# Cached sliding-window attention on one core: three pairs of value tiles loaded as 32 KB rows, and a new order of the loads

## The chip, the cores and the metric

One core of one Trainium2 chip runs the whole program. The metric is the device time of one execution in microseconds (us); the span of a profile is the part of it between first and last instruction, some 1.8 us shorter. A run of a program on one core repeats within some 0.3 us here, so most experiments were timed in five rounds beside the kernel before on the same chip. All ratios are the mean time of one kernel's fast runs over that of the other's of the same rounds, so not quite the ratio of the medians that are quoted. A run over 1.5% above the fastest of its kernel counts as slow, the others as fast; slow runs are named and left out of the times.

## The reference, cut to what matters

One decoding step of grouped-query attention over the last 512 positions of a cache: 32 batches, 32 query heads, 8 key-value heads, head size 128, bf16.

```python
W = min(4096, max(256, Sk // 4))                      # 512
q = (x @ wq).reshape(B, Sq, Hq, Dh) ...               # [32, 32, 1, 128]
k = repeat(k_cache[:, :, Sk - W:, :], 4, axis=1)
v = repeat(v_cache[:, :, Sk - W:, :], 4, axis=1)
p = softmax(einsum("bhqd,bhkd->bhqk", q, k) * Dh ** -0.5)
o = einsum("bhqk,bhkd->bhqd", p, v)
out = o.transpose(...).reshape(B, Sq, Hq * Dh) @ wo   # [32, 1, 512]
```

33.5 MB of K, 33.5 MB of V, 4.2 MB of wq and 4.2 MB of wo have to be read once, 75.5 MB in all, for very little arithmetic.

## The kernel before: what the change touches

K and V are cut into 16 tiles each of 2 MB: 128 rows (batch, head, quarter of the window) of 16 KB, one row per partition. Tile 2q+1 continues the rows of tile 2q, so two tiles of one pair are 32 KB in a row in memory. There are three K buffers and four V buffers. One queue (SyncE, SP) issues all loads but the small x in a fixed order; an issue waits until its buffer is free. K needs its two transposes on VectorE (T) before its buffer is free; V needs its 64 matmuls on TensorE.

Every load of 128 rows leaves 16 completion increments in the trace, as many as the page counts DMA engines; they are read here as one from each engine when its share has landed. The first is that of the earliest engine, the last that of the latest; their distance is called the spread here. Steps are counted from one load's first increment to the next one's. An engine that took no instruction fetch is called undisturbed.

```python
NK = 3
NV = 4
DMA_ORDER = (
    "K0 K1 K2 V0 K3 K4 V1 K5 K6 K7 V2 K8 K9 V3 K10 V4 K11 K12 V5 K13 K14 V6 K15 V7 V8 V9 V10 V11 V12 "
    "V13 V14 V15"
).split()
# ... PE_ORDER, DVE_ORDER, ACT_ORDER: fixed orders of the compute steps (cut)

def cache_rows(cache, m):
    q, e = divmod(m, 2)
    rows = cache[4 * q:4 * q + 4, :, SK - W:, :].rearrange("b g (s r) d -> (b g) s (r d)", s=KS)
    return rows[:, :, e * CR * DH:(e + 1) * CR * DH]

@block.sync
def _(sp):
    sp.dma_start(w_sb[:, 2:4, :]..., wq_rows[:, wq_half:]).then_inc(sem_wq[1], 16)   # second half of wq
    for name in DMA_ORDER:
        n = int(name[1:])
        if name[0] == "K":
            if n >= NK:
                sp.wait_ge(dve_T, 2 * (n - NK + 1))
            sp.dma_start(K_sb[:, n % NK]..., cache_rows(k_cache, n)).then_inc(sem_k[n % NK], 16)
        else:
            if n >= NV:
                sp.wait_ge(pe_PV, n - NV + 1)
            sp.dma_start(V_sb[:, n % NV]..., cache_rows(v_cache, n)).then_inc(sem_v[n % NV], 16)
    sp.wait_ge(pe_PV, 2 * Z_HOME.rindex("w") + 2)
    # ... nine loads of wo, the output store (cut)

def pv(m):                                  # TensorE, one value tile
    # ... (cut)
    pe.wait_ge(sem_v[m % NV], 16 * (m // NV + 1))
    for r in range(CR):                     # CR = 64
        ins = pe.matmul(O_ps[:, q % 2, 0:P], lhsT=V_sb[:, m % NV, r, :], rhs=z_of(q)[:, :, x0 + r, :],
                        start=(e == 0 and r == 0), stop=(e == 1 and r == CR - 1), tile_position=(0, 0))
    ins.then_inc(pe_PV, 1)
```

## Time and profile before

| | kernel before |
|---|---|
| time, median | 187.69 us (3 runs), 187.67 us over 6 runs |
| span of the profiled execution | 185.9 us |
| DMA packets | 6304, 75.80 MB |
| one 2 MB transfer behind another, undisturbed engine | 4.893 us |
| eighth of nine wo transfers, named by the chain, and ninth landed | 182.67 and 182.99 us |
| first and last of the 16 DMA engines at the end | 3.2 us apart |

### The profile page before, as it was taken

The page shows a single profiled execution, that of the slowest core. Times are in us where ns is not written, and L with a number is a line of the kernel's source. Part 1 is how long each engine was busy: PE and PEld are TensorE (multiplying, and loading weights), DVE is VectorE, ACT ScalarE, POOL GpSimd, SP SyncE. Part 2 cuts the span into 40 slices and gives each one's busy share as a digit, 9 for nine tenths or more (in the row PEclk, how much of TensorE's full clock was granted, in tenths as well). Part 3 has the DMA queues.
Part 4 walks back from the last instruction along what each step waited for, and adds up shares of the span by engine and source line. Part 5 has one row for each costly group of instructions (what it writes and reads, how often), then busy time and mean ns, then how long its engine had stood idle before and what let it go on. Part 6 is the DMA issues. An engine that isn't in the chain of part 4 may idle for free.

```text
span 185.9 us, 3842 instructions
## 1 busy us (share of the span) xinstructions
PE 109.0 (59%) x1604; PEld 89.4 (48%) x1604; DVE 131.9 (71%) x239; ACT 82.3 (44%) x142; POOL 32.0 (17%) x82
## 2 busy tenths in 40 slices
PE   0232004336179906929906994159979975998752
PEld 0100001022069805819606974019949975987741
DVE  0006999689999999993699987999999995010001
ACT  3001000269320397020695018925998999910011
POOL 7100390500700080060240041000040000000000
PEclk9999999955557985885985599576999999999998
DMA  6999999999999999999999999999999999999980
GB/s 194 434 448 412 437 423 423 448 412 437 420 416 441 416 427 434 416 437 427 423 421 423 441 423 420 434 423 430 428 412 434 427 423 430 420 423 411 405 332 27
DMA packets 6304, 75.80 MB, mean 408 GB/s; under 512 B 720, under 2 KB 912, under 8 KB 1936
## 3 DMA queue, kind: packets, MB, share of 16 engines
q1 hardware_dynamic: 6240, 75.53, 96.4%
q8 instruction: 12, 0.20, 0.4%
q10 hardware_dynamic: 48, 0.03, 0.1%
q14 instruction: 4, 0.03, 0.0%
HBM read 75.53 MB, written 0.03 MB: 406 GB/s over the span
## 4 chain that ended last, share of the span: by engine, by line
DMA 64%; DVE 20%; PE 9%; issue 3%; SPq 3%; DVEq 0%
DMA V_sb<-in_v_cache_dram 31%; DMA K_sb<-in_k_cache_dram 14%; DMA w_sb<-in_wo_dram 12%; DVE KT_sb L431 12%; PE O_ps L356 8%; DMA w_sb<-in_wq_dram 6%; DVE w_sb L453 4%; DVE QA_sb L421 2%; SPq L214 2%; PE X_ps L299 1%; SPq L202 1%; DVE oT_sb L414 0%; DVE KT_sb L409 0%; PE X_ps L393 0%; DVE maxv L438 0%
## 5 line engine op out<-in xcount | busy, mean ns | idle before, releaser
L431 DVE STREAM_TRANSPOSE KT_sb<-K_sb 128x2048 uint32<-128x2048 uint32 x32 | 72.3, 2287 | 1.3 <-DMA K_sb<-in_k_cache_dram 1.1
L356 PE MATMUL O_ps<-w_sb,V_sb 128*128 128x128 bf16 x640 | 47.0, 244 | 9.6 <-DVE w_sb L453 5.0
L356 PEld LDWEIGHTS O_ps<-w_sb,V_sb 128*128 128x128 bf16 x640 | 45.6, 110 | 12.3 <-DVE w_sb L453 6.5
L268 POOL COPY QBD<-QA_sb 32x64 bf16<-32x64 bf16 x64 | 25.6, 540 | 81.2 <-PE S_ps L319 63.6
L520 ACT ACTIVATE w_sb<-PTc,mask 128x512 bf16<-128x512 bf16 x60 | 38.9, 729 | 0.0
L319 PE MATMUL S_ps<-KT_sb,QBD 128*32 128x512 bf16 x256 | 20.7, 475 | 26.6 <-DVE KT_sb L431 20.2
L453 DVE TENSOR_SCALAR w_sb<-PTc,mask 128x512 bf16<-128x512 bf16 x100 | 30.2, 370 | 6.3 <-PE O_ps L356 6.3
L319 PEld LDWEIGHTS S_ps<-KT_sb,QBD 128*32 128x32 bf16 x256 | 7.5, 110 | 36.5 <-issue 32.4
L492 ACT ACTIVATE X_ps<-S_ps,negmax 128x512 f32<-128x512 f32 x8 | 5.3, 657 | 42.8 <-DVE negmax L440 42.8
L338 PE MATMUL PT_ps<-P_bf,pick 128*128 128x128 bf16 x128 | 11.4, 260 | 17.9 <-ACT P_bf L501 14.7
L338 PEld LDWEIGHTS PT_ps<-P_bf,pick 128*128 128x128 bf16 x128 | 9.8, 119 | 20.9 <-ACT P_bf L501 16.3
L530 ACT ACTIVATE oT_sb<-O_ps 128x128 bf16<-128x128 f32 x8 | 6.0, 750 | 28.2 <-PE O_ps L356 28.2
L356 PE MATMUL O_ps<-K_sb,V_sb 128*128 128x128 bf16 x256 | 14.9, 217 | 3.5 <-DMA V_sb<-in_v_cache_dram 2.2
L356 PEld LDWEIGHTS O_ps<-K_sb,V_sb 128*128 128x128 bf16 x256 | 14.5, 96 | 4.3 <-issue 2.5
L520 ACT ACTIVATE K_sb<-PTc,mask 128x512 bf16<-128x512 bf16 x24 | 15.3, 725 | 1.6 <-DVE KT_sb L431 1.6
L453 DVE TENSOR_SCALAR K_sb<-PTc,mask 128x512 bf16<-128x512 bf16 x40 | 12.1, 377 | 0.3 <-ACT PTc L511 0.2
L474 DVE CAST K_sb<-S_ps 128x256 bf16<-128x256 f32 x1 | 0.4, 425 | 14.3 <-PE S_ps L368 14.3
L356 PE MATMUL O_ps<-KT_sb,V_sb 128*128 128x128 bf16 x128 | 7.5, 217 | 2.3 <-DMA V_sb<-in_v_cache_dram 2.3
L356 PEld LDWEIGHTS O_ps<-KT_sb,V_sb 128*128 128x128 bf16 x128 | 7.3, 96 | 2.5 <-issue 2.5
L520 ACT ACTIVATE KT_sb<-PTc,mask 128x512 bf16<-128x512 bf16 x12 | 7.7, 728 | 0.0
L501 ACT ACTIVATE P_bf<-X_ps,recip 128x512 bf16<-128x512 f32 x8 | 5.5, 684 | 4.5 <-DVE recip L446 4.4
L409 DVE CAST KT_sb<-X_ps 128x512 bf16<-128x512 f32 x1 | 0.7, 692 | 9.2 <-PE X_ps L299 9.2
(41 smaller groups left out, 49.6 us busy)
## 6 DMA issues: line engine op xcount, KB each, us to landing
K_sb<-in_k_cache_dram SPq DMA_DIRECT2D x16, 2048.0 KB, 15.1
V_sb<-in_v_cache_dram SPq DMA_DIRECT2D x16, 2048.0 KB, 16.8
w_sb<-in_wq_dram SPq DMA_DIRECT2D x2, 2048.0 KB, 9.7
w_sb<-in_wo_dram SPq DMA_DIRECT2D x7, 512.0 KB, 19.8
w_sb<-in_wo_dram SPq DMA_DIRECT2D x1, 384.0 KB, 22.6
w_sb<-in_wo_dram SPq DMA_DIRECT2D x1, 128.0 KB, 14.4
oT_sb<-in_x_dram ACTq DMA_DIRECT2D x1, 32.0 KB, 4.4
out_dram<-oT_sb SPq DMA_DIRECT2D x1, 32.0 KB, 1.5
```

What stands on the lines that cost most here:

```text
L214: sp.dma_start(wo_sb[:, hg, i0:i1].rearrange("p i n -> p (i n)"), wo[hg * 512:(hg + 1) * 512, :].rearrange("(m i) n -> m (i n)", i=4)[:, i ...
L268: pool.tensor_copy(dst[:, i, :, x0:x0 + 4], src).then_inc(pool_qbd, 1)
L319: ins = pe.matmul(S_ps[32 * c:32 * c + 32, q % 2, :], lhsT=QBD[:, q % 2, g, b, e, :], rhs=bass.AP(tensor=KT_sb, offset=s0 * slot + (b * G ...
L338: ins = pe.matmul(PT_ps[:, r, :], lhsT=pick[:, r, KS - s:KS - s + P], rhs=P_bf[:, s, :], start=(s == 0), stop=(s == KS - 1), tile_position ...
L356: ins = pe.matmul(O_ps[:, q % 2, 0:P], lhsT=V_sb[:, m % NV, r, :], rhs=z_of(q)[:, :, x0 + r, :], start=(e == 0 and r == 0), stop=(e == 1 a ...
L421: dve.tensor_copy(QA[32 * a:32 * a + 32, c], QW[32 * c:32 * c + 32, :, :, a::4].rearrange("p h k q -> p h q k"),).then_inc(dve_q, 1)
L431: dve.transpose(KT_w[:, n % NK, b].rearrange("p i r s -> p r i s"), K_w[:, n % NK, :, 32 * b:32 * b + 32],).then_inc(dve_T, 1)
L453: ins = dve.tensor_scalar(z_of(q)[:, k].rearrange("p x r -> p (x r)"), PTc[:, q % RING].rearrange("p x r -> p (x r)"), mask[:, k:k + 1], N ...
L492: act.activation(P_f32, S_ps[:, q % 2, :], ACTF.Exp, bias=negmax[:, q:q + 1], scale=SCALE, accum_out=sums[:, q:q + 1],).then_inc(act_exp, 1)
L501: act.activation(P_bf[:, :, :], P_f32.rearrange("p (x s) -> p s x", s=KS), ACTF.Copy, scale=recip[:, q:q + 1],).then_inc(act_P, 1)
L520: ins = act.activation(z_of(q)[:, k].rearrange("p x r -> p (x r)"), PTc[:, q % RING].rearrange("p x r -> p (x r)"), ACTF.Copy, scale=mask[ ...
L530: act.activation(oT_sb[:, :, 4 * q:4 * q + 4].rearrange("p h a -> p a h"), O_ps[:, q % 2, 0:P].rearrange("p (a h) -> p a h", a=4), ACTF.Co ...
```

## The change

Its intent: fewer, longer packets for six of the value tiles. V0+V1, V4+V5 and V6+V7 become one transfer each. The second half of wq ("B0") goes behind K0, the query block ("Q0") on VectorE behind the transposes of K0, and all orders are sorted anew around that.

```diff
     DMA_ORDER = (
-        "K0 K1 K2 V0 K3 K4 V1 K5 K6 K7 V2 K8 K9 V3 K10 V4 K11 K12 V5 K13 K14 V6 K15 V7 V8 V9 V10 V11 V12 "
-        "V13 V14 V15"
+        "K0 B0 K1 K2 K3 V0 K4 K5 K6 V2 K7 K8 V3 K9 K10 K11 V4 K12 K13 K14 V6 K15 V8 V9 V10 V11 V12 V13 V14 "
+        "V15"
     ).split()
...  (PE_ORDER, DVE_ORDER, ACT_ORDER sorted anew, same steps; cut)
+    V_PAIRED = (0, 4, 6)
...
-        def cache_rows(cache, m):
+        def cache_rows(cache, m, k=1):
...
-            return rows[:, :, e * CR * DH:(e + 1) * CR * DH]
+            return rows[:, :, e * CR * DH:(e + k) * CR * DH]
...
-                    if n >= NV:
-                        sp.wait_ge(pe_PV, n - NV + 1)
+                    k = 2 if n in V_PAIRED else 1
+                    if n + k > NV:
+                        sp.wait_ge(pe_PV, n - NV + k)
                     sp.dma_start(
-                        V_sb[:, n % NV].rearrange("p r d -> p (r d)"), cache_rows(v_cache, n)
+                        V_sb[:, n % NV:n % NV + k].rearrange("p a r d -> p (a r d)"), cache_rows(v_cache, n, k)
                     ).then_inc(sem_v[n % NV], 16)
...
-                pe.wait_ge(sem_v[m % NV], 16 * (m // NV + 1))
+                if m - 1 not in V_PAIRED:
+                    loads = sum(1 for k in range(m % NV, m + 1, NV) if k - 1 not in V_PAIRED)
+                    pe.wait_ge(sem_v[m % NV], 16 * loads)
...  (the query block becomes a step "Q0" of DVE_ORDER: "T0.0 T0.1 Q0 T1.0 ..."; cut)
```

## The prediction

> **What bounds the kernel now.** I read the page top down (busy shares, slices, DMA queues), then the chain of waits for what ended last, then windows of 1 us over the tail, then the queue's own waits, and last the trace's records of single DMA packets and of the completion increments of each transfer (16 per transfer, one per DMA engine).
>
> ```profile
> span 185.9 us, 3842 instructions
> PE 109.0 (59%) x1604; PEld 89.4 (48%) x1604; DVE 131.9 (71%) x239; ACT 82.3 (44%) x142; POOL 32.0 (17%) x82
> DMA  6999999999999999999999999999999999999980
> ...
> q1 hardware_dynamic: 6240, 75.53, 96.4%
> q8 instruction: 12, 0.20, 0.4%
> ```
>
> No compute engine is above 71%; the 16 DMA engines are at nine tenths from the second slice to the last but two. 75.53 MB pass on one queue. The second thing to see is the small q8 row: 12 packets, 0.20 MB, that fetch instructions and run on the same DMA engines.
>
> ```profile
> 160.04 22.62 DMA w_sb<-in_wo_dram
> 182.67 0.04 issue
> 182.71 0.59 PE X_ps L393 x16
> 183.30 0.02 issue
> 183.32 0.28 DVE oT_sb L477
> ```
>
> The chain ends in the last wo transfer landing at 182.67, then 0.6 us of matmul, the copies and the output store: about 3.2 us to the end of the span. So the end is the last byte plus a constant.
>
> ```profile
> 178.00:179.00 1.00, 0.48 (x28) 0.36 (x27) 0.42 (x1) 0.00 (x0) 0.00 (x0) 1.00 1.04 410
> 179.00:180.00 1.00, 1.00 (x76) 0.85 (x64) 0.00 (x0) 0.00 (x0) 0.00 (x0) 1.00 0.80 311
> 180.00:181.00 1.00, 0.43 (x20) 0.23 (x16) 0.00 (x0) 0.00 (x0) 0.00 (x0) 1.00 0.61 227
> 181.00:182.00 1.00, 0.25 (x16) 0.23 (x16) 0.00 (x0) 0.00 (x0) 0.00 (x0) 1.00 0.22 85
> 182.00:183.00 1.00, 0.45 (x24) 0.18 (x12) 0.00 (x0) 0.00 (x0) 0.00 (x0) 1.00 0.09 31
> ```
>
> The last two columns are DMA share and GB/s: the rate doesn't stop, it runs down over 3 us. The 16 engines finish at different times. The completion increments say the same: the 16 increments of one transfer lie 0.37 us apart up to 48 us, 1.9 us apart from 54 us, and 3.3 us apart from 155 us to the end. The steps are single engines falling back by about 1.55 us, at the times of the q8 packets (47.6, 63.5, 78.1, ... 151.9, 162.9, 172.0); at the last three of these an engine that was already late falls back again. So three engines with two instruction fetches each set the end, about 3.2 us behind the earliest. An engine without a fetch takes one 2 MB transfer every 4.893 us (step from one transfer's first increment to the next), which is 428.6 GB/s for sixteen.
>
> From the packet records: median 614 ns for 16384 B, 160 ns for 4096 B, 46 ns for 1024 B, 9 ns for a completion packet. Between 4 KB and 16 KB it is 454 ns for 12288 B, or 27.1 GB/s per engine; 4096 B at that rate are 151 ns, so about 8.7 ns are fixed per packet.
>
> [...]
>
> **The change part by part.**
> 1. Three pairs, V0+V1, V4+V5, V6+V7, become one transfer each of 128 rows of 32 KB in place of two of 128 rows of 16 KB. Bytes are unchanged. Per DMA engine and pair: 16 data packets become 8 and two completion packets become one. If one row is one packet, as at 16 KB, a 32 KB packet should take 2 x 614 - 8.7 = 1219 ns (an estimate), so a pair saves 8 x 8.7 + 9 = 79 ns per engine. Three pairs: 0.24 us. This lies wholly on the path that sets the end, since the late engines carry the same share of rows.
> 2. The second half of wq goes from second to third place, behind K0. Bytes and total are the same. First increments in order of issue come near 8, 12.9, 17.8 us; so K0 lands near 13.3 and the wq half near 18.2. DVE turns K0 (two transposes, 4.5 us) from 13.3 to 17.8 while it waits; PE then needs 1.9 us, to 20.1; the query block (0.69 + 0.71 + 16 x 0.3) takes DVE to about 26.4. Before, the query block ended at 21.5 and the K0 transposes at 26.04. So DVE stands where it stood, 0.4 us later. Worth 0 at the end; but K0's buffer comes free at 17.8, not 26.0, so K3 is issued 8 us earlier.
> 3. The orders on PE, DVE and ACT are re-sorted; the counts of matmuls, transposes and copies are the same. Three PE waits go. DVE ended its last product at 156.1 and PE consumes the last value tile only when it lands near 173, so shifts of a few us there are hidden: 0.
> 4. The tail, V8 to V15 as singles and then wo, is untouched: 0.
>
> Sum: -0.24 us of 187.69, or 187.45. I put 187.4[...].
>
> **The rivals.**
> A. The queue runs dry: a pair needs two free buffers, so its issue waits for one more value step, and K transfers stand behind it on the same sequencer.
>
> ```profile
> SPq L202 <- DVE KT_sb L431: 94.6, 13, 21.6
> SPq L208 <- PE O_ps L356: 40.7, 7, 17.9
> ```
>
> These long waits look alarming but run while transfers are queued. K7 is the tightest now: issued near 53.0, with K6 before it finishing on the fastest engine near 56.9, so 3.9 us in hand; others have 6 us and more. After: K3 at about 17.8 against 27.6 for what precedes it; K4 near 31 against 42; K6 near 41 against 52; K7 near 53 against 62. V4's pair needs V1 consumed (63.5 before, asked for about 80); V6's needs V3 consumed (89.8 before, asked for about 107). Nothing gets near zero. A miss would cost what the gap lasts, 1 to 4 us, and part would be regained by no one. I give it one chance in twenty.
> B. The hardware cuts a 32 KB row into two packets of 16 KB or less. Then only the three completion packets go, 0.03 us: 187.65. No packet above 16384 B is in the trace, so this is open; one in four.
> C. Instruction fetches fall otherwise. They cost one engine 1.55 us each, six times the whole expected gain. If a late engine caught a third[...], the end moves +0.3 to +1.5 us[...]. If fewer engines were hit twice, -1.5 us. Against it: the PE program keeps its order of size and the fetches seem to go round the same engines, so the three late engines should stay late. One in eight for anything over 0.3 us.
> D. Compute becomes the end: V15 lands near 173, its matmuls, copies and selection end near 178.7, and the first wo products end near 180, against 182.67 for the last wo. 2 us of slack; 0.24 us doesn't use it up.
>
> **Range and chances.** The centre is 187.4. B puts it at 187.65, [...]C at 188 or more or under 187. 8 in 10: 186.8 to 188.0. 2% is 3.75 us; nothing in the sum comes near it. Faster by that would need more than the whole spread of the engines removed; slower would need a dry queue. So 1%, 97%, 2%.
>
> **What would show each step.** Packets of 32768 B near 1219 ns and 384 fewer of 16 KB pairs' halves (768 become 384); a pair's first increment 9.71 us after the transfer before it, not 9.79; the last wo landing near 182.4; the spread at the end still near 3.3 us with 12 fetches; DMA at nine tenths throughout, and the query copies after two transposes, ending near 26.4. The prediction is wrong if a slice shows the DMA share down in mid-run, if the end spread changes, or if 32 KB packets run at another rate than 27 GB/s.

The sum came to -0.24 us of 187.69, or 187.45, all of it from the packet records; the forecast was put 0.05 us lower, at 187.4. From the trace of the kernel before: the 12 packets of q8 are 16384 B each and took 1.02 to 1.10 us, and the data packet next to each of the first ten took 1.08 to 1.17 us in place of 0.61.

## More of the kernel before

The busy shares, the end of the chain, the tail and the queue's waits are shown in the prediction. One more view is needed later: the issuing queue in order of time, at the start (start, duration of the group of issues, queue, line, out<-in, count; L161 and L194 are the halves of wq, L202 is K, L208 is V).

```profile
0.80 0.40 SPq L161 DMA_DIRECT2D w_sb<-in_wq_dram  x1
1.26 0.42 SPq L194 DMA_DIRECT2D w_sb<-in_wq_dram  x1
1.72 2.00 SPq L202 DMA_DIRECT2D K_sb<-in_k_cache_dram  x3
3.77 0.60 SPq L208 DMA_DIRECT2D V_sb<-in_v_cache_dram  x1
26.04 4.92 SPq L202 DMA_DIRECT2D K_sb<-in_k_cache_dram  x2
```

Six transfers of 2 MB are handed over in the first 4 us. The next issue, K3, must wait for K0's buffer and comes at 26.04. The transfer before it in the queue, V0, gave its first completion increment at 32.4, so 6.4 us of work were still in the queue.

## The result, and the profile after

187.37 us (6 runs, 187.29 to 187.53) beside 187.67 us for the kernel before (187.29 to 187.85): ratio 0.9988, 95% interval 0.9975 to 1.0001. A second measurement in later rounds (below, e10) gave 0.9988 again, 0.9975 to 1.0002. Each interval just touches 1, so the gain of about 0.28 us is seen twice but is small beside the scatter of single runs. The trace shows its parts much more sharply than the clock does.

The page of the changed kernel:

```profile
span 185.5 us, 3839 instructions
DMA  6999999989999999999999999999999999999980
...
q1 hardware_dynamic: 5808, 75.53, 96.4%
q8 instruction: 12, 0.20, 0.4%
```

The data queue has 432 packets fewer, 6240 to 5808: 384 data packets and 48 completion packets, as three pairs make. The DMA row is as full as before. The 12 instruction fetches are still there.

The end of its chain of waits, answering to the lines from 160.04 of the kernel before:

```profile
161.16 21.09 DMA w_sb<-in_wo_dram
182.25 0.04 issue
182.30 0.65 PE X_ps L397 x16
182.97 0.28 DVE oT_sb L482
```

It is the same end, a wo transfer and a constant, and the landing at 182.25 lies 0.42 us before that of the kernel before (182.67). The tail in windows of 1 us (last two columns: DMA share, GB/s):

```profile
179.00:180.00 1.00, 0.57 (x44) 0.40 (x31) 0.00 (x0) 0.00 (x0) 0.00 (x0) 1.00 0.68 268
180.00:181.00 1.00, 0.41 (x16) 0.23 (x16) 0.00 (x0) 0.00 (x0) 0.00 (x0) 1.00 0.51 186
181.00:182.00 1.00, 0.41 (x16) 0.23 (x16) 0.00 (x0) 0.00 (x0) 0.00 (x0) 1.00 0.18 69
```

The run-down over 3 us is unchanged. And the queue at the start (L203 is K now, L197 the wq half, L210 V):

```profile
0.80 0.39 SPq L161 DMA_DIRECT2D w_sb<-in_wq_dram  x1
1.25 0.61 SPq L203 DMA_DIRECT2D K_sb<-in_k_cache_dram  x1
1.90 0.89 SPq L197 DMA_DIRECT2D w_sb<-in_wq_dram  x1
2.83 15.53 SPq L203 DMA_DIRECT2D K_sb<-in_k_cache_dram  x3
18.41 0.60 SPq L210 DMA_DIRECT2D V_sb<-in_v_cache_dram  x1
```

K3 and the first pair are issued by 19.0 us. K2, which stands before K3, gives its first increment at 27.5, so K3 has 9.6 us in hand in place of 6.4.

What the trace's packet and completion records say of the two kernels (us from the span's start; "first" and "last" of the 16 increments of one transfer):

```
                                        before              changed
packet of 16384 B, median               614 ns  (x4352)     613 ns  (x3584)
packet of 32768 B, median               none                1218 ns (x384)
step of a single tile (first incr.)     4.89                4.89
step of a pair (first incr.)            2 x 4.893 = 9.79    9.71, 9.71, 9.71
first half of wq, first                 7.94                7.88
V15, first / last                       169.50 / 172.85     169.12 / 172.40
last wo, first / last                   179.78 / 182.99     179.41 / 182.57
```

From the first half of wq to V15 the undisturbed engine takes 161.24 us in place of 161.56.

### The profile page after: what moved, and what is told of

Same layout as the page of the kernel before. It is cut to its first block, busy times and chain, and to the rows that moved or that the text cites. A ratio compares the mean times of both kernels' runs of the same rounds, so it can differ in the third digit from the quotient of the medians.

```text
span 185.5 us, 3839 instructions
## 1 busy us (share of the span) xinstructions
PE 110.9 (60%) x1604; PEld 90.7 (49%) x1604; DVE 132.4 (71%) x239; ACT 81.9 (44%) x142; POOL 32.4 (17%) x82
## 3 DMA queue, kind: packets, MB, share of 16 engines
q1 hardware_dynamic: 5808, 75.53, 96.4%
## 4 chain that ended last, share of the span: by engine, by line
DMA 41%; PE 22%; DVE 19%; ACT 7%; issue 6%; SPq 3%; DVEq 0%
PE O_ps L360 15%; DMA V_sb<-in_v_cache_dram 12%; DMA w_sb<-in_wo_dram 11%; DVE KT_sb L436 10%; DMA K_sb<-in_k_cache_dram 9%; DMA w_sb<-in_wq_dram 9%; DVE w_sb L458 5%; PE S_ps L321 4%; ACT w_sb L525 4%; DVE QA_sb L426 2%; SPq L216 2%; ACT KT_sb L525 1%; PE PT_ps L340 1%; DVE maxv L443 1%; PE X_ps L301 1%
## 5 line engine op out<-in xcount | busy, mean ns | idle before, releaser
L436 DVE STREAM_TRANSPOSE KT_sb<-K_sb 128x2048 uint32<-128x2048 uint32 x32 | 72.5, 2291 | 10.5 <-DMA K_sb<-in_k_cache_dram 10.4
L458 DVE TENSOR_SCALAR w_sb<-PTc,mask 128x512 bf16<-128x512 bf16 x100 | 31.8, 386 | 2.2 <-ACT PTc L516 1.1
L321 PE MATMUL S_ps<-KT_sb,QBD 128*32 128x512 bf16 x256 | 21.5, 490 | 18.1 <-POOL QBD L270 11.0
L340 PE MATMUL PT_ps<-P_bf,pick 128*128 128x128 bf16 x128 | 12.6, 277 | 24.1 <-ACT P_bf L506 19.6
L340 PEld LDWEIGHTS PT_ps<-P_bf,pick 128*128 128x128 bf16 x128 | 10.9, 128 | 28.1 <-ACT P_bf L506 22.7
L458 DVE TENSOR_SCALAR K_sb<-PTc,mask 128x512 bf16<-128x512 bf16 x40 | 10.7, 344 | 2.4 <-ACT PTc L516 2.4
L301 PE MATMUL X_ps<-w_sb,oT_sb 128*32 128x512 bf16 x32 | 3.8, 627 | 10.6 <-DMA w_sb<-in_wq_dram 10.6
L491 ACT ACTIVATE KT_sb<-X_ps 128x512 bf16<-128x512 f32 x1 | 0.6, 597 | 17.4 <-PE X_ps L301 17.4
L443 DVE TENSOR_REDUCE maxv<-S_ps 128x1 f32<-128x512 f32 x8 | 5.5, 683 | 3.7 <-PE S_ps L321 3.7
```

Source lines behind the costliest of these rows:

```text
L301: ins = pe.matmul(X_ps[32 * c:32 * c + 32, k, :], lhsT=xT_sb[:, kt, :], rhs=w_sb[:, kt, c * 1024 + k * 512:c * 1024 + (k + 1) * 512], star ...
L321: ins = pe.matmul(S_ps[32 * c:32 * c + 32, q % 2, :], lhsT=QBD[:, q % 2, g, b, e, :], rhs=bass.AP(tensor=KT_sb, offset=s0 * slot + (b * G ...
L340: ins = pe.matmul(PT_ps[:, r, :], lhsT=pick[:, r, KS - s:KS - s + P], rhs=P_bf[:, s, :], start=(s == 0), stop=(s == KS - 1), tile_position ...
L436: dve.transpose(KT_w[:, n % NK, b].rearrange("p i r s -> p r i s"), K_w[:, n % NK, :, 32 * b:32 * b + 32],).then_inc(dve_T, 1)
L443: dve.tensor_reduce(maxv[:, q:q + 1], S_ps[:, q % 2, :], AX.X, ALU.max).then_inc(dve_sm, 1)
L458: ins = dve.tensor_scalar(z_of(q)[:, k].rearrange("p x r -> p (x r)"), PTc[:, q % RING].rearrange("p x r -> p (x r)"), mask[:, k:k + 1], N ...
```

## The experiments

### e1: the new orders without the pairs

```diff
-    "K0 B0 K1 K2 K3 V0 K4 K5 K6 V2 K7 K8 V3 K9 K10 K11 V4 K12 K13 K14 V6 K15 V8 ...
+    "K0 B0 K1 K2 K3 V0 V1 K4 K5 K6 V2 K7 K8 V3 K9 K10 K11 V4 V5 K12 K13 K14 V6 V7 K15 V8 ...
-    V_PAIRED = (0, 4, 6)
+    V_PAIRED = ()
```

> All orders of the changed kernel, but the three pairs issued as two 16 KB-row transfers each, back to back. Theory (the gain is the fixed cost per packet, three pairs, 0.24 us; the order is worth nothing): the time of the kernel before, 187.67, ratio to it 1.000. Rival (the earlier K0, or a fuller queue, brings the gain): 187.37, ratio 0.9984, as the whole change.

Measured: 187.69 us (187.54 to 187.96) beside 187.60; ratio 1.0003, 0.9990 to 1.0016. As the theory had it: the orders alone gain nothing. The intervals of e1 and of the changed kernel overlap, so the clock alone doesn't tell the two apart; the traces do. In e1 the three pairs, as singles back to back, take 9.79, 9.75 and 9.79 us, in the changed kernel 9.71 each. In its trace V15's first increment is at 169.46, where the kernel before has 169.50 and the changed one 169.12.

### e2: the pairs in the old orders

```diff
-    "K0 K1 K2 V0 K3 K4 V1 K5 K6 K7 V2 K8 K9 V3 K10 V4 K11 K12 V5 K13 K14 V6 K15 V7 V8 V9 ...
+    "B0 K0 K1 K2 V0 K3 K4 K5 K6 K7 V2 K8 K9 V3 K10 V4 K11 K12 K13 K14 V6 K15 V8 V9 ...
+    V_PAIRED = (0, 4, 6)
     (query block first on VectorE, all other orders as before)
```

> All orders of the kernel before, with the three pairs put at the places of V0, V4 and V6. Theory (packets): the whole gain, ratio 0.9985, with a pair's first increment 9.71 us after the transfer before it and packets of 32768 B at 1.218 us. Rival (order): ratio 1.000 though the packets are there.

Measured: 190.63 us (190.05 to 191.84), ratio 1.0166, 1.0141 to 1.0192. Both expectations missed. The packets were there (384 of 32768 B at 1218 ns, steps of 9.71 us), but the kernel is 3.0 us slower than before. The windows from 55 to 60 us show where, first the changed kernel, then e2:

```profile
55.00:60.00 5.00, 5.00 (x83) 5.00 (x81) 5.00 (x3) 0.00 (x0) 0.00 (x0) 0.89 1.01 429
```

```profile
55.00:60.00 5.00, 2.70 (x24) 2.44 (x25) 5.00 (x10) 1.28 (x2) 0.89 (x2) 0.51 0.51 174
```

The DMA engines stand still for half of these 5 us (DMA share 0.51 in place of 1.01). The queue of e2 (L204 is K, L211 V) and its largest group on VectorE (after the second bar: the idle time ahead of the transposes, and what ended it):

```profile
26.37 32.04 SPq L204 DMA_DIRECT2D K_sb<-in_k_cache_dram  x5
58.45 0.60 SPq L211 DMA_DIRECT2D V_sb<-in_v_cache_dram  x1
...
L437 DVE STREAM_TRANSPOSE KT_sb<-K_sb 128x2048 uint32<-128x2048 uint32 x32 | 72.3, 2288 | 11.7 <-DMA K_sb<-in_k_cache_dram 11.7
```

The pair reads V1 two places earlier, and so K3 and K4 land later: K3's last increment comes at 42.86 in place of 37.68. VectorE, which needs them, waits 11.7 us for K where the page before had 1.1 (the changed kernel waits 10.4 us as well, but 7.3 of them for K0 at the very start), everything after shifts, and K7 is issued near 57.9, not 53.0. What precedes it, K6, gives its increments between 56.74 and 58.61. For the early engines the queue is empty; K7's first increment comes 8.28 us after K6's in place of 4.89. So the rival that the prediction had called "the queue runs dry" is real, and the changed kernel, with the same pairs in the new order, has no such gap.

### e8: the changed kernel with wq and the query block back in front

```diff
-    "K0 B0 K1 K2 K3 V0 ...          -    "T0.0 T0.1 Q0 T1.0 ...
+    "B0 K0 K1 K2 K3 V0 ...          +    "Q0 T0.0 T0.1 T1.0 ...
```

> The changed kernel with only the second half of wq put back before K0 and the query block put back before the first transposes. Theory (what the new order is for is a full queue: K3 and the first pair are asked for when K0's buffer comes free, 18 us with K0 second and 26 us with K0 third, while what precedes them is read by about 27): the queue is all but dry once, a gap of 0.2 to 1 us at K3, 187.5 to 188.3. Rival (the place of wq is free once the pairs stand where they do): 187.37.

Measured: 188.24 us (188.03 to 188.78), ratio 1.0030, 1.0017 to 1.0043; so 0.87 us slower than the changed kernel, inside what the theory gave. The window from 25 to 30 us, first of the changed kernel, then of e8:

```profile
25.00:30.00 5.00, 0.00 (x0) 0.00 (x0) 4.84 (x7) 0.00 (x0) 3.15 (x10) 1.00 0.99 423
```

```profile
25.00:30.00 5.00, 0.00 (x0) 0.00 (x0) 5.00 (x3) 0.00 (x0) 2.79 (x8) 1.00 0.91 341
```

K3 was issued near 26 with K2 ending at 27.4, and the step to K3's first increment is 5.70 us in place of 4.89: a gap of 0.81 us, and 0.87 us in the time. Handing K3 over 1.4 us before the queue is empty is thus too late. This is what moving wq and the query block does for the change.

### e4 and e5: more pairs

```diff
e4  -    V_PAIRED = (0, 4, 6)      "... K6 V2 K7 K8 V3 K9 ... K15 V8 V9 V10 V11 V12 ... V15"
    +    V_PAIRED = (0, 2, 4, 6, 8, 10)   "... K6 V2 K7 K8 K9 ... K15 V8 V10 V12 V13 V14 V15"
e5  +    V_PAIRED = (0, 4, 6, 8, 10, 12, 14)   "... K15 V8 V10 V12 V14"
```

> The changed kernel with three pairs more (V2, V8, V10), V12 to V15 single. Theory (packets): another 3 x 79 ns = 0.24 us, so about 187.13, ratio to the kernel before 0.997. Rival (the pairs' gain doesn't add up, or the wait for two free buffers opens a gap in the queue at V10, asked for near 136 with some 5 us of queue in hand): 187.4 or more, with a step between landings longer than 9.71 us.

Measured: 189.29 us (188.65 to 190.06, five fast runs; a sixth, 192.39, was slow), ratio 1.0092, 1.0071 to 1.0113. The theory's sum failed and its rival held. Every pair takes its 9.70 to 9.71 us, but two steps are longer than they should be: K11 5.93 us in place of 4.89, and V10's pair 11.41 us in place of 9.71, because it waits for V7 to be consumed. Three pairs more would have given 0.24 us; two gaps cost 1.0 and 1.7 us on the early engines. The traced run, the fastest, lost less than that, because the late engines catch up in a gap: its spread at the end is 1.7 us in place of 3.2.

> Pairs to the very end (V12 and V14 too, V2 single). Theory (the queue stays full only while a pair's buffers come free before the queue is drained): V12's pair waits for V9 to be consumed near 150, when the queue holds only the rest of V10's pair, landing near 151, so about a gap of 1 to 2 us, and the last two value tiles come together near 172, so their matmuls (7.6 us) end near 180 and the selection near 182: 188 to 190 us. Rival (no waits matter, packets alone): 7 pairs, 187.05.

Measured: 193.52 us (192.98 to 194.21), ratio 1.0314, 1.0295 to 1.0333. The direction was as expected, the size was not: the gap at V12's pair is not 1 to 2 but 15.64 - 9.71 = 5.9 us (and one of 0.5 us stands at V10's pair). The window from 150 to 155 us, and then the end of the chain of waits of e5:

```profile
150.00:155.00 5.00, 5.00 (x93) 5.00 (x90) 4.97 (x20) 3.97 (x8) 0.00 (x0) 1.00 0.19 52
```

```profile
153.53 13.76 DMA V_sb<-in_v_cache_dram
...
172.56 1.32 PE X_ps L371 x16
173.88 10.83 PE O_ps L359 x192
184.74 0.73 ACT oT_sb L534
```

The pair was issued at 153.53, when V9 was consumed and the queue had been empty since the last increment of V10's pair at 151.5. TensorE had the two tiles of V8's pair to do one after the other, with the scores in between, so it was later than 150. And the chain now ends on TensorE: V14 and V15 arrive together, and their matmuls and what follows them set the end, not the landing of wo. So singles at the end are the better choice here: a single tile can be worked on while the next is read.

The gaps of these runs side by side (first increments, us):

```
                      issued before its        gap    sum
                      predecessor's end
e5, V12's pair              -3.7               5.9    2.2
e2, K7                      -1.1               3.4    2.3
e4, V10's pair               0.6               1.7    2.3
e8, K3                       1.4               0.8    2.2
e5, V10's pair               1.95              0.5    2.4
```

The sum hardly changes: an issue needed some 2.2 to 2.4 us of queue in front of it, and what was missing became a gap. Two cases of e4 don't fit: K11 had 2.7 us and lost 1.0 all the same, V13 had 2.5 and lost 0.2, and no run says why. With 3.1 us and more no K or V load of a fast trace lost over 0.12 us; the least in the changed kernel is 4.3 us, at V10.

### e3: the fixed cost per packet, by making more of them

```diff
-    sp.dma_start(K_sb[:, n % NK]..., cache_rows(k_cache, n)).then_inc(sem_k[n % NK], 16)
+    for h in range(2):
+        sp.dma_start(K_sb[:, n % NK, h * CR // 2:(h + 1) * CR // 2]...,
+                     cache_rows(k_cache, n)[:, :, h * CR * DH // 2:(h + 1) * CR * DH // 2]).then_inc(sem_k[n % NK], 16)
-    dve.wait_ge(sem_k[n % NK], 16 * (n // NK + 1))
+    dve.wait_ge(sem_k[n % NK], 32 * (n // NK + 1))
```

> The changed kernel with each of the 16 K tiles loaded as two transfers of 8 KB rows, so 16 x 8 data packets and 16 completion packets more per DMA engine, at the same bytes. Theory (a fixed cost per packet of 8.7 ns on the path that sets the end): 16 x 79 ns = 1.26 us later, 188.6, packets of 8192 B at about 311 ns. Rival (the fixed cost is hidden in the pipelining of packets): 187.4. A K transfer's step is then 4.97 us in place of 4.89.

Measured: the four fast runs lie at 188.43 to 188.69, median 188.51 us, ratio 1.0043, 1.0030 to 1.0056; against 187.37 for the changed kernel (of other rounds) this is 1.14 us more, 71 ns per K tile where 79 were expected; by the two ratios to the kernel before it is 1.0 us. A fifth run, the profiled one, took 241.8 us and counts as slow; it isn't used for times. Its matmuls were slower (322 ns in the largest group, 244 in the changed kernel) with a full granted clock in the records; no run explains it. Up to 60 us its transfers keep the usual pace, and there a 1 MB half takes 2.48 us, a tile 4.96 us in place of 4.89, and 8192 B packets a median of 309 ns. So the fixed cost is real and lies on the path, about 71 / 9 = 8 ns per packet. (There is no fast trace of e3 past 60 us.)

### e6 and e9: fewer instruction fetches

Both leave out matmuls, and load, wait and order everything as the changed kernel does. Their outputs are wrong, which doesn't matter for the times.

```diff
e6  +    nr = CR // 2 if m < 12 else CR
e9  +    nr = CR // 2
    -    for r in range(CR):                     ... stop=(e == 1 and r == CR - 1)
    +    for r in range(nr):                     ... stop=(e == 1 and r == nr - 1)
```

> Wrong on purpose: the changed kernel with half of the value matmuls of V0 to V11 left out, 384 matmuls with their weight loads, so 768 PE instructions or three blocks of 16 KB less. Loads, orders and waits are unchanged. Theory (the end is set by the three DMA engines that get two instruction fetches): 9 fetches in place of 12, no engine hit twice before the end, the end spread near 1.9 us in place of 3.2, and about 1.3 us less: 186.0. Rival (the spread belongs to the engines or to the data): the spread stays at 3.2 us and the time at 187.4, as PE is not on the path.

The three blocks are an estimate from the trace of the kernel before: 12 fetches of 16384 B for 3208 PE instructions, one for 267.

Measured: 187.33 us (187.12 to 187.57), ratio 0.9981: no gain over the changed kernel, so the expected 186.0 failed. The reason is in the trace. The page has

```profile
q8 instruction: 9, 0.15, 0.3%
```

and the spread of the engines stood at 2.0 us up to the wo transfer that landed at 180.16, as the theory wants. Then the ninth fetch began at 179.7, and the next transfer's last increment came 2.02 us after the one before, where the same step is 0.96 in e9: spread 3.05 us. The ninth fetch had come just before the end, on an engine that was late already. This was an argument after the fact, so it was tried again with one block less.

> Wrong on purpose: as e6, but half of the value matmuls of all 16 tiles left out, 512 matmuls, 1024 PE instructions, four blocks of 16 KB less than the changed kernel. In e6 the end spread was 2.0 us until the ninth and last fetch, at 179.7 us, made one engine late that had been late before, and the last increment jumped from 2.0 to 3.05 us behind the first. Theory (the end is set by an engine with a second fetch): 8 fetches, no engine hit twice, the spread stays near 2.0 us to the end and the last output-weight landing comes 1.0 to 1.2 us earlier than in the changed kernel, 186.2 to 186.4. Rival (the last transfers spread whatever the fetches do): spread 3 us, 187.35.

Measured: 186.17 us (186.00 to 186.33), ratio 0.9919, 0.9906 to 0.9933, just under what was expected. The count and the tail of e9:

```profile
q8 instruction: 8, 0.13, 0.3%
```

```profile
179.00:180.00 1.00, 0.48 (x16) 0.21 (x8) 0.00 (x0) 0.00 (x0) 0.00 (x0) 0.50 0.63 237
180.00:181.00 1.00, 0.62 (x16) 0.35 (x16) 0.00 (x0) 0.00 (x0) 0.00 (x0) 0.50 0.33 117
181.00:182.00 1.00, 0.62 (x16) 0.36 (x16) 0.26 (x1) 0.26 (x1) 0.00 (x0) 0.50 0.00 0
```

The run-down is over at 181, a whole microsecond before that of the changed kernel; the spread at the end is 1.93 us and the last wo increment at 181.34 in place of 182.57. The chain ends on a wo landing in both runs (182.19 in e6, 181.03 in e9, and the ninth transfer 0.3 us later), so the shorter matmuls themselves set nothing; yet 1024 PE instructions fewer, and with them 8 fetches in place of 12, gain 1.2 us: the fetches share the DMA engines (the data packet next to one took 1.08 to 1.17 us in place of 0.61 in the kernel before). e6 and e9 differ by one fetch and 1.16 us, though on two chips, on which the kernel before differs by 0.07 us. (e9's last matmuls ran at a granted clock of 0.50, which is against it, not for it: from 181 to 182 us 16 of them took 0.62 us, in the changed kernel at 1.00 0.41.)

### e7: which engines are late

The last block of wo was issued first of the nine and cut into transfers of 15, 14, ... 2 rows and one of 9.

> The changed kernel with the last output-weight block issued first of the nine and cut into transfers of 15, 14, ... 2 and 9 rows, to see from the completion increments which engines are late: a transfer of n rows should use n engines. Theory (three engines with two fetches each, about 3.2 us late, the same from run to run): each drop from n to n-1 rows takes one time out of the set of increments, and the three late ones leave at fixed n. No claim on the time beyond 187 to 190, because small transfers cost issue time.

191.1 us, correct. That a transfer of n rows uses n engines was the assumption before the run. The records agree: each transfer has one early record and n late ones. The late ones, in us from the span's start:

```
rows
 10   170.80 171.22 171.28 171.34 171.99 172.33 174.22 175.17 175.67 175.95
  9   171.19 171.49 171.59 171.59 172.26 172.57 174.45 175.94 176.21
  8   171.46 171.75 171.95 172.53 172.84 174.68 176.20 176.43
  7   171.71 172.04 172.78 173.07 174.92 176.41 176.64
  6   172.00 172.35 173.01 173.31 175.15 176.62
  5   172.31 172.60 173.24 173.54 175.43
```

From each row to the next all times move by about 0.3 us and one drops out. The three latest drop out from 10 to 9, from 7 to 6 and from 6 to 5 rows; which engines these are, no record says. So only a transfer of 5 rows or fewer was free of all three, and it had lost eight of the earlier ones too; no version that evens out the load was built. The last wo increment comes at 185.29, 2.7 us later than in the changed kernel; what the small transfers add to that (their 15 issues took 5.57 us) was not taken apart.

### e10: the changed kernel once more

> The changed kernel once more, to narrow its interval beside the runs of the kernel before on this chip. Theory (three pairs, 0.24 us): ratio 0.9987, 187.37. Rival (no gain, the first ratio of 0.9988 was chance): 1.000.

Measured: 187.41 us (187.27 to 187.59) beside 187.69; ratio 0.9988, 0.9975 to 1.0002. No run with a correct result beat the changed kernel.

## Why the prediction was right or wrong

**Bound and end: right.** The time is the last byte plus a constant: the wo landings moved by 0.42 us and the span by 0.4. One reading was off: the landing at 182.67, which the view names, is that of the eighth of nine wo transfers. The ninth, of 128 KB, landed at 182.99, and the last four matmuls began at 183.03, so it sets the end; it too came 0.42 us earlier in the changed kernel (182.57).

**Part 1, the pairs, 0.24 us: right, and shown.** A 32 KB row is one packet (384 of them); 1218 ns measured, 1219 estimated; a pair steps 9.71 us, as written. The rival that the hardware cuts the rows in two (one in four) is out. The measured gain is 0.28 to 0.30 us in the medians and 0.32 us in the trace; three times 9.79 - 9.71 are 0.22 of it. The other 0.1 us of the trace is one step of the kernel before, K7 with 4.98 us in place of 4.89. Single steps 0.1 us too long also stand in e1 (K13), e8 (K11) and e9 (K10), so it is not the change's. e1 shows that the shorter step goes when only the pairs go, and e3 shows the same cost at five times the size, 8 ns per packet.

**The extra for longer reads: not seen.** The 187.4 had a few hundredths for a better rate; 32 KB packets run at the rate of the others (1218 ns for 32768 B, 613 ns for 16384 B). That the measured 187.37 lies on 187.4 and not on the 187.45 of the sum is scatter, not a confirmation.

**Part 2, wq behind K0: its times right, its worth misread.** The transposes of K0 began at 13.30 and the query block ended at 26.43, as worked out. But "Worth 0 at the end" is true only without the pairs (e1). With them the early release of K0's buffer keeps the queue full: 0.87 us without it (e8).

**Part 3, the sorted orders, "0": right alone, wrong as a reading of the change.** The prediction counted the parts as if each stood by itself. They don't: pairs in the old order cost 3.0 us (e2).

**Rival A, the dry queue: right for this change, but measured against the wrong limit.** The estimated distances held: K3 at 18, its predecessor near 27.5. But "nothing gets near zero" takes zero as the limit, and the gaps put it at 2.2 to 2.4 us; by the prediction's limit e8, with 1.4 us in hand, would have been safe. In e2, e4, e5 and e8 each time a gap opened, and in e2 and e8 its size on the early engines (3.4 and 0.8 us) is about what the time lost (3.0 and 0.87).

**Rival C, the instruction fetches: the mechanism shown, the danger not met.** 12 fetches and 3.2 us of spread both before and after. e6 and e9 show that one more fetch late in the run moves the end by 1.05 to 1.2 us; that it fell on an engine with an earlier one, and that the three latest engines had two each, is read from the times, as no record names the engine of a packet.

**Rival D, compute as the end: right, not met here.** Only e5, with V14 and V15 in one transfer, ended on TensorE.

## What to carry to other kernels

When one queue is full from start to end, count what each packet costs beside its bytes (about 8 ns here, e3), but before making transfers longer work out for every issue how much is still in the queue at that moment; an issue that came less than 2.2 to 2.4 us before the end of its predecessor cost more here than the packets gave. A longer transfer asks for its buffers earlier and landed later here, so it wanted an order of its own (3.0 us lost in the old one, e2), and at the end of the stream it left the consumer with too much at once (193.52 us, e5). And where the DMA engines finish at different times, look at what else runs on them: here the fetches of TensorE's own program set the last microsecond (8 in place of 12: 186.17 us in place of 187.41, e9, with a wrong result).
